# A fused linear-attention and mixer kernel on one core: the first batch's value tiles from GpSimd's DMA queue

## The chip, the cores and the metric

The kernel runs on one core of a Trainium2 chip. A core has TensorE (PE in the profile; PEld are its weight loads), VectorE (DVE), ScalarE (ACT), GpSimd (POOL) and SyncE (SP), which run side by side and wait for each other by semaphores. Transfers between the chip's memory (HBM) and the core's on-chip memory are issued by one of these engines and carried out by 16 DMA engines. The metric is device microseconds (us) of one execution; times are medians of several runs.

## The reference

Two blocks follow each other. The first is a gated linear attention over 4 batches, 8 heads, 768 steps and 48 channels:

```python
f = 1.0 / (1.0 + np.exp(-f_logit))
for t in range(S):
    state = f[:, :, t, :, None] * state + np.einsum('bhd,bhe->bhde', k[:, :, t], v[:, :, t])
    y[:, :, t] = np.einsum('bhd,bhde->bhe', q[:, :, t], state)
```

The second takes its output, as 4 x 768 x 384, through a low-rank mixing of the steps and two dense layers:

```python
u  = x + (x.transpose(0, 2, 1) @ U @ V).transpose(0, 2, 1)      # U 768x32, V 32x768
ch = np.maximum(u @ w_ch1, 0.0) @ w_ch2                         # 384x1536, 1536x384
out = u + ch
```

The inputs q, k, v and f_logit are float32. The weights arrive in a 64-bit form and are converted on the core.

## The kernel before

A unit is one pair of heads of one batch; there are 16, and units 0 to 3 (HP is 4) are the first batch. For each unit the kernel loads the gate logits f, the keys k, the queries q and the values v. The values go into tiles of their own, of which three exist; f, k and q go into two slots that alternate, so unit n+2 reuses what unit n has read:

```python
v_tiles[n] = three.tile([P, NBL, 2, D], F32, name="v_nat")
nat[n % 2][nm]                     # slots "late" (even units) and "other" (odd units)

def load(n, *names):
    b, hp = divmod(n, HP)
    for nm in names:
        if nm == "v":
            v_tiles[n] = three.tile([P, NBL, 2, D], F32, name="v_nat")
        for par in range(2):                       # the two heads of the pair
            head = src[nm][b, 2 * hp + par]
            if nm == "v" and par:
                for s in range(2):                 # the second head's halves are swapped: two transfers
                    nc.sync.dma_start(
                        out=v_tiles[n][(1 - s) * C : (2 - s) * C, :, par, :],
                        in_=head.rearrange("(c s p) d -> s p c d", s=2, p=C)[s],
                    )
                continue
            if nm == "v" or n < TURNED:
                dst = v_tiles[n] if nm == "v" else nat[n % 2][nm]
                nc.sync.dma_start(out=dst[:, :, par, 0:D], in_=head.rearrange("(c p) d -> p c d", p=P))
                continue
            # ... later units: finer transfers in another layout

load(0, "f", "k", "q")
load(1, "f")
load(0, "v")
load(1, "k", "q", "v")
```

A transfer of one head is 128 partitions by 6 rows of 48 float32, so it is made of pieces of 192 bytes. After these loads GpSimd fills constants and clears buffers, ending with a few small ones:

```python
nc.gpsimd.memset(added[:, 0:1], 0.0)
for i in range(2):
    nc.gpsimd.memset(wholes[i][:, 0:1], 0.0)
```

The work on a unit has these parts:

```python
# front of a unit
pt = on_tensor("f")                                  # TensorE transposes f into a PSUM tile
nc.scalar.activation(halves(f)[:, :, :, 1:C], pt[:, :, :, 1:C], AF.Sigmoid)
nc.vector.tensor_tensor_scan(...)                    # suffix products of the gates (keep)
nc.vector.tensor_tensor(halves(t), on_tensor("k"), halves(T["X"]), ALU.mult)
nc.vector.tensor_tensor_scan(Y, f[:, 0:S], starts, 0.0, ALU.mult, ALU.add)
nc.vector.tensor_tensor(halves(t), on_tensor("q"), halves(T["Y"]), ALU.mult)
# rear of a unit
nc.tensor.transpose(...)                             # kept: the keys back, by chunks
nc.tensor.matmul(ds[...], lhsT=T["kb"][...], rhs=vt[...])      # states: keys by VALUES
nc.vector.tensor_tensor_scan(states, added, whole, 0.0, ALU.add, ALU.mult)
nc.tensor.matmul(sc[...], lhsT=T["k"][...], rhs=T["q"][...])   # scores
nc.vector.tensor_tensor(T["A"], sc, causal, ALU.mult)
nc.tensor.matmul(y[...], lhsT=T["q"][...], rhs=T["st"][...])   # read
nc.tensor.matmul(y[...], lhsT=T["A"][...], rhs=vt[...])        # inner: scores by VALUES
```

The first batch's units follow each other in this loop, which also issues the later loads; the order of TensorE, VectorE and ScalarE is kept as written, and a scheduler places SyncE's and GpSimd's instructions:

```python
for n in range(HP):
    pieces = front(n, "keep", "keys") + rear(n - 1, "scan", "scores")
    pieces += [lambda: busy(3)] + rear(n, "kept") + front(n, "read_back", "queries")
    if n + 1 < HP:
        pieces += front(n + 1, "gates") + rear(n - 1, "read", "inner") + rear(n, "states")
    for piece in pieces:
        piece()
    if n < 2:
        load(n + 2, "v")
    if n == 1:
        for start, _ in weights[: early + 2]:        # U, V and two blocks of w_ch1
            start()
    elif n > 1:
        load(n + 2, "f", "k", "q", "v")
```

f, k and q of unit n+2 are loaded as soon as unit n has read its own. busy(3) are three matmuls without use, to keep TensorE occupied. Each weight is loaded, then converted by two ScalarE, three VectorE and one GpSimd operation (lines 90 to 95). Each load on a queue has one of eight semaphores, and waits for the load that had the semaphore before.

## Time and profile before

| What | Value |
|---|---|
| Time, median of 3 runs | 488.54 us (488.51 to 489.53) |
| Span of the profiled execution | 486.9 us |
| TensorE granted clock | 0.998 of full |
| DMA moved | 34.34 MB, mean 71 GB/s |
| DMA pieces under 512 B | 149206 of 158679 |
| Value loads v_nat | 16 of 144 KB, 32 of 72 KB, all from SyncE |
| Small clearings on GpSimd end | 5.4 us |
| GpSimd idle after them | 36.87 us, until the first weight is converted at 42.29 us |

The page has busy times by engine, the span in 40 slices with a digit for the busy tenths of each, the DMA queues, the chain of work that ended last, and groups of instructions. In the table of stretches DMA's share can pass 1, since pieces of a transfer overlap in an engine. In the timeline a line gives start, length, engine, source line, operation, output and inputs, and in brackets the idle time before it and what ended it. "issue" stands for idle time in which the engine waited for nothing that the profile shows. SPq is SyncE's queue of transfers; its times are those of the issue, and the data land later.

### The profile page before, as it was taken

The numbers are of one execution on the slowest core, as the hardware profiler recorded it, in microseconds if no ns is written. First come the engines' busy times: TensorE is split into PE (matmuls) and PEld (weight loads), VectorE is DVE, ScalarE is ACT, GpSimd is POOL, SyncE is SP. The second block draws the span as 40 slices with busy tenths as digits, with TensorE's granted clock in tenths as the row PEclk, the third lists the DMA queues.
The fourth block names the chain that finished last, engine by engine and source line by source line (L and its number), as shares of the span: only waits on it lengthen the run. The fifth ranks groups of instructions, "written<-read, shape, count | busy, mean of one in ns | idle before, by whom it ended". The sixth has DMA issues, their size and how long they took to land.

```text
span 486.9 us, 12734 instructions
## 1 busy us (share of the span) xinstructions
PE 469.2 (96%) x5541; PEld 400.0 (82%) x5541; DVE 355.4 (73%) x563; ACT 163.2 (34%) x309; POOL 37.6 (8%) x49
## 2 busy tenths in 40 slices
PE   7996899999999999999999999999999999999995
PEld 4775688886566568899898888899979999999995
DVE  5887689777999857656857548797896886958642
ACT  2444666664334313423231403433231312112200
POOL 3002245453000000000000000000000000000000
PEclk9999999999999999999999999999999999999999
DMA  9979975756778512333535100100000000000001
GB/s 146 158 153 178 254 194 135 162 143 79 110 116 121 96 41 36 52 48 67 76 55 94 25 18 18 27 3 20 19 1 1 33 2 18 16 1 34 1 33 38
DMA packets 158679, 34.34 MB, mean 71 GB/s; under 512 B 149206, under 2 KB 157078, under 8 KB 158614
## 3 DMA queue, kind: packets, MB, share of 16 engines
q1 hardware_dynamic: 158614, 33.44, 37.0%
q8 instruction: 45, 0.74, 0.6%
q14 instruction: 20, 0.16, 0.1%
HBM read 28.70 MB, written 4.72 MB: 69 GB/s over the span
## 4 chain that ended last, share of the span: by engine, by line
PE 79%; DVE 10%; DMA 3%; issue 3%; ACT 2%; SPq 2%; DVEq 0%; ACTq 0%
PE pw L312 26%; PE pz L258 23%; PE pp L410 11%; PE y L863 2%; PE pt L660 2%; PE sc L788 2%; PE ds L825 2%; PE y L881 2%; PE po L283 2%; PE idle L962 2%; PE put L246 1%; DMA late<-in_f_logit_dram 1%; DVE late L694 1%; DVE late L712 1%; PE pt L809 1%
## 5 line engine op out<-in xcount | busy, mean ns | idle before, releaser
L258 PE MATMUL pz<-uT,w 128*128 128x256 f32 x504 | 115.7, 383 | 0.3 <-ACT uT L247 0.3
L258 PEld LDWEIGHTS pz<-uT,w 128*128 128x128 f32 x504 | 93.4, 190 | 13.3 <-issue 0.5
L312 PE MATMUL pw<-w,z_all 128*128 128x192 f32 x216 | 37.7, 329 | 0.0
L312 PE MATMUL pw<-zw,w_raw 128*128 128x192 f32 x216 | 37.4, 327 | 0.0
L312 PEld LDWEIGHTS pw<-zw,w_raw 128*128 128x128 f32 x216 | 35.2, 190 | 0.8 <-issue 0.6
L312 PEld LDWEIGHTS pw<-w,z_all 128*128 128x128 f32 x216 | 35.0, 190 | 0.7
L95 POOL TENSOR_TENSOR w<-w_y,w_r 128x384 int32<-128x384 int32 x24 | 31.5, 1311 | 41.5 <-DVE w_y L94 36.5
L694 DVE TENSOR_TENSOR_SCAN late<-fz,late 128x768 f32<-128x768 f32 x16 | 28.1, 1755 | 8.9 <-ACT fz L689 4.2
L268 ACT ACTIVATE z_all<-pz 128x512 f32<-128x512 f32 x33 | 19.7, 596 | 41.4 <-PE pz L258 41.3
L410 PE MATMUL pp<-v_nat,late 128*128 128x128 f32 x224 | 28.8, 275 | 0.0
L712 DVE TENSOR_TENSOR_SCAN late<-fz,other 128x768 f32<-128x768 f32 x16 | 27.9, 1745 | 0.1
L410 PEld LDWEIGHTS pp<-v_nat,late 128*128 128x128 f32 x224 | 27.0, 192 | 0.0
L283 PE MATMUL po<-w,zw 128*128 128x384 f32 x72 | 25.6, 499 | 0.0
L283 PE MATMUL po<-w,z_all 128*128 128x384 f32 x72 | 25.3, 496 | 0.3 <-DVE o L187 0.3
L403 ACT ACTIVATE other<-other 128x512 f32<-128x512 f32 x18 | 11.3, 631 | 39.9 <-DVE other L187 39.9
L851 ACT COPY st<-added 128x576 f32<-128x576 f32 x12 | 14.7, 1224 | 27.5 <-DVE added L846 27.5
L92 DVE TENSOR_SCALAR w_y<-w_y 128x384 f32<-128x384 f32 (+3 forms) x27 | 13.1, 485 | 14.0 <-ACT w_y L90 13.8
L795 DVE TENSOR_TENSOR A<-sc,causal 128x768 f32<-128x768 f32 x16 | 15.2, 947 | 10.7 <-PE sc L788 10.7
L283 PEld LDWEIGHTS po<-w,z_all 128*128 128x128 f32 x72 | 13.1, 190 | 8.7 <-DVE o L187 0.9
L283 PEld LDWEIGHTS po<-w,zw 128*128 128x128 f32 x72 | 12.9, 189 | 8.7 <-issue 1.2
L187 DVE TENSOR_TENSOR w_raw<-z_all 128x768 f32<-128x768 f32 x12 | 11.4, 954 | 10.6 <-ACT z_all L268 9.2
L312 PE MATMUL pw<-w,other 128*128 128x192 f32 x108 | 18.6, 327 | 0.0
(193 smaller groups left out, 825.6 us busy)
## 6 DMA issues: line engine op xcount, KB each, us to landing
w_raw<-in_moe_w_ch_dram SPq DMA_DIRECT2D x18, 384.0 KB, 3.9
out_dram<-o SPq DMA_DIRECT2D x24, 192.0 KB, 1.9
v_nat<-in_v_dram SPq DMA_DIRECT2D x16, 144.0 KB, 3.6
v_nat<-in_v_dram SPq DMA_DIRECT2D x32, 72.0 KB, 3.3
zw<-in_moe_w_ch_dram SPq DMA_DIRECT2D x6, 384.0 KB, 5.7
late<-in_f_logit_dram SPq DMA_DIRECT2D x10, 96.0 KB, 3.1
late<-in_k_dram SPq DMA_DIRECT2D x10, 96.0 KB, 3.0
late<-in_q_dram SPq DMA_DIRECT2D x10, 96.0 KB, 2.6
```

Source lines behind the costliest of these rows:

```text
L92: nc.vector.tensor_scalar(f, f, SMALLEST, LARGEST, ALU.max, ALU.min)
L95: nc.gpsimd.tensor_tensor(dst.bitcast(I32), shaped(y.bitcast(I32)), shaped(r), ALU.add)
L187: nc.vector.tensor_tensor(*args)
L258: nc.tensor.matmul(pm[:, i * 2 * P : (i + 1) * 2 * P], lhsT=w1[:, m, o : o + P], rhs=uT[a][:, m, :], start=(m == 0), stop=(m == NDC - 1))
L268: nc.scalar.activation(z[a, c][:, k : k + 2, :].rearrange("p i t -> p (i t)"), pm, AF.Relu)
L283: nc.tensor.matmul(pm, lhsT=z[a, i // NI][:, i % NI, s * P : (s + 1) * P], rhs=w2[:, i, :], start=(i == 0), stop=(i == NFC - 1))
L312: nc.tensor.matmul(pm[:, n * HM : (n + 1) * HM], lhsT=lhs[:, i, :], rhs=rhs[:, i, :], start=(i == 0), stop=(i == NI - 1))
L410: nc.tensor.matmul(pm[:, i, r * P : (r + 1) * P], lhsT=room["w"](wn)[:, r * P : (r + 1) * P], rhs=x_node(a, xn), start=((xn, wn) == of[0]) ...
L694: nc.vector.tensor_tensor_scan(backwards(X, S - 1, S), backwards(f, S, S), backwards(ends, S - 1, S), 0.0, ALU.mult, ALU.add,)
L712: nc.vector.tensor_tensor_scan(Y, f[:, 0:S], starts, 0.0, ALU.mult, ALU.add)
L795: nc.vector.tensor_tensor(T["A"], sc[:, :, 0 : NBL * C].rearrange("p h (c i) -> p h c i", i=C), causal.unsqueeze(1).unsqueeze(1).broadcast ...
L851: nc.scalar.copy(st, states.rearrange(by_e, c=NCH))
```

## The change

The value tiles of units 0 to 3 are issued from GpSimd instead of SyncE, twelve transfers in all. Those of units 0 and 1 are moved behind GpSimd's clearings in the program, so that they don't hold these up; those of units 2 and 3 are called where they were. All else stays with SyncE, whose queue now has fewer loads in front of the f, k and q that follow. The sizes and the layout of the transfers are the same.

```diff
+            queue = nc.gpsimd if nm == "v" and n < HP else nc.sync
             for par in range(2):
                 head = src[nm][b, 2 * hp + par]
                 if nm == "v" and par:
                     for s in range(2):
-                        nc.sync.dma_start(
+                        queue.dma_start(
                             out=v_tiles[n][(1 - s) * C : (2 - s) * C, :, par, :],
                             in_=head.rearrange("(c s p) d -> s p c d", s=2, p=C)[s],
                         )
                     continue
                 if nm == "v" or n < TURNED:
                     dst = v_tiles[n] if nm == "v" else nat[n % 2][nm]
-                    nc.sync.dma_start(out=dst[:, :, par, 0:D], in_=...)
+                    queue.dma_start(out=dst[:, :, par, 0:D], in_=...)
                     continue
...
     load(0, "f", "k", "q")
     load(1, "f")
-    load(0, "v")
-    load(1, "k", "q", "v")
+    load(1, "k", "q")
...
     for i in range(2):
         nc.gpsimd.memset(wholes[i][:, 0:1], 0.0)
+    load(0, "v")
+    load(1, "v")
```

The lines of the kernel below the change move down by two or three.

## The prediction

> **What bounds the kernel now.** I read the page first, then the table of stretches, then the chain of work that ended last in order of time up to 60 us, then the timeline of the same stretch. From the page:

> ```profile
> PE 469.2 (96%) x5541; PEld 400.0 (82%) x5541; DVE 355.4 (73%) x563; ACT 163.2 (34%) x309; POOL 37.6 (8%) x49
> ...
> DMA  9979975756778512333535100100000000000001
> ...
> q8 instruction: 45, 0.74, 0.6%
> ```

> TensorE is busy nearly throughout; DMA is full only in the first slices (12.2 us each). The twelve value transfers that change queue all lie there. In the table of stretches TensorE is busy for 61.67 of the 62 us from 55 to 117, and after 117 us the DMA share is 0.23. So only the first 55 us matter, and what is won or lost in them should move the end by as much. The same table for the start (stretch, length, busy us and counts of PE, PEld, DVE, ACT and POOL, clock, DMA share, GB/s):

> ```profile
> 5.00:10.00 5.00, 4.61 (x16) 3.33 (x15) 2.78 (x5) 1.59 (x4) 0.42 (x6) 1.00 1.49 170
> 10.00:15.00 5.00, 5.00 (x82) 3.68 (x80) 3.43 (x4) 2.40 (x5) 0.00 (x0) 1.00 1.46 165
> 15.00:20.00 5.00, 4.49 (x74) 2.94 (x73) 4.93 (x8) 1.36 (x4) 0.00 (x0) 1.00 1.23 160
> 20.00:25.00 5.00, 4.72 (x174) 4.16 (x175) 4.65 (x7) 2.73 (x7) 0.00 (x0) 1.00 0.78 133
> 25.00:30.00 5.00, 5.00 (x82) 3.59 (x78) 4.90 (x5) 1.60 (x3) 0.00 (x0) 1.00 0.88 149
> ```

> Two things are to be seen. DMA moves 165 to 170 GB/s until about 15 us with a share above 1, so it is full: a second queue cannot make it faster, only reorder it. And from 15 us VectorE is busy for 4.65 to 4.93 of each 5 us, so the units of batch 0 go at VectorE's pace (its suffix scans start at 14.47, 22.34 and 30.71 us: some 8 us a unit), as long as no load comes late. One load is at that edge, in the chain:

> ```profile
> 14.68 5.21 DMA late<-in_f_logit_dram
> 19.89 0.14 issue
> 20.02 0.85 PE pt L660 x6
> ```

> Unit 2's gate logits are issued from SyncE at 14.09 and 14.68 us, land at 19.89, and TensorE transposes them 0.13 us later. The timeline shows how near the other conditions are:

> ```profile
> 19.99 0.64 PEld L660 LDWEIGHTS pt<-ident,late 128*128 128x128 f32 x6 [0.74 <-DVE A L795]
> 20.02 0.85 PE L660 MATMUL pt<-ident,late 128*128 128x128 f32 x6 [0.53 <-DMA late<-in_f_logit_dram]
> ...
> 20.90 0.80 ACT L681 ACTIVATE fz<-pt 128x756 f32<-128x756 f32 x1 [0.59 <-PE pt L660]
> ...
> 22.34 1.75 DVE L694 TENSOR_TENSOR_SCAN late<-fz,late 128x768 f32<-128x768 f32 x1
> ```

> The sigmoid ends at 21.70 us and VectorE takes the scan at 22.34, when it has finished its product of the queries (21.46 plus 0.96 us). So unit 2's gates have 0.64 us of slack and no more. The value tiles have little either: unit 0's are first read at 13.46 us (state matmuls, L825), and their transfers are issued at 6.25 to 8.80 us and take 3.8 to 4.7 us to land.

> Later there are two holes on TensorE with no cause that the profile names:

> ```profile
> 42.13 0.74 PE L788 MATMUL sc<-qT,kz 48*64 48x64 f32 x34 [1.72 <-issue]
> ...
> 46.86 1.16 PE L208 MATMUL ph<-x,U 128*32 128x288 f32 x11 [1.94 <-issue]
> ```

> I take them for waits for TensorE's instructions. The page's q8 carries 45 pieces and 0.74 MB, about 16 KB each; 2 x 5541 matrix instructions over 45 are some 246 to a piece; and by the table of stretches TensorE starts 127 matmuls and 127 weight loads from the end of the first hole to that of the second. The matmuls here are small, so a piece is used up in a few us.

> [...]

> **The change part by part.** Removed from SyncE: 12 issues; those of units 0 and 1 take 0.81, 1.69, 0.84 and 1.49 us in SyncE's timeline, 4.8 together, so some 9.7 us for four units. That is no time on the path by itself, since SyncE's issues were slow because DMA was full.

> Added on GpSimd: 12 issues, starting after its last small memset at about 5.4 us. It is idle from there to 42.29 us (its first weight addition waited 36.87 us), so the issuing itself costs nothing there. I have no duration for it; I assume 0.7 to 1.5 us each. Units 0, 1 and 2 follow without a wait; unit 3 waits for unit 0's tile, which is free at about 23.2 us.

> Moved: the built order of SyncE's instructions. Before, it is (f0 is f of unit 0) f0 k0 q0 f1 v0 k1 q1 v1 f2 k2 q2 f3 v2 k3 q3 v3, then U, V and the first layer's weights. After, it is f0 k0 q0 f1 k1 q1 U f2 k2 V q2 f3 k3, three blocks of weights, q3, then f4. The scheduler has filled the gaps with weights. So two kinds of bytes come ahead of f2 that were behind it: U, and unit 2's values, which GpSimd hands out early.

> The sum for f2: one tensor of one unit is 2 x 144 KB, 0.295 MB. Before, nine of them end with f2: 2.65 MB. At 165 GB/s that is 16.1 us; DMA starts at about 1.8 us, so 17.9, and f2 landed at 19.89, so 2.0 us are latency. After, if the two queues share evenly from about 7 us, 1.38 MB of SyncE's (f1 k1 q1 U f2) stand beside 0.885 MB of GpSimd's (v0 v1 v2), which is the smaller, so all of it is done first. Thus 0.197 MB (U) and 0.295 MB (v2) are added: 0.49 MB / 165 GB/s = 3.0 us. f2 lands at 22.9, the slack of 0.64 is used up, and unit 2's scan is 2.3 us late. VectorE has no room to win that back before 40 us.

> Other loads by the same count: k1 at about 15.2 instead of 13.5 us; its product on VectorE runs at 16.63, the transposes need 0.9, so it just fits. q2, f3, k3 and q3 come to 27.7, 30, 33 and 38 us against needs (2.3 us later than before) of 30.6, 31.2, 35.1 and 39.5. They fit. v0, handed out from 5.4 to 9 us and sharing, lands at 13 to 14.5 against 13.46; a lag of about 1.4 us is swallowed, since the next VectorE work that depends on what follows is at 16.63.

> At 36 to 47 us the loads differ from before: more weights are in by then, with larger pieces, so the instruction fetches may have to wait less. Of the 3.7 us of holes I count 0.5 to 1 us won, but with little confidence, as the same bytes still have to come before about 55 us. Weights themselves gain nothing: ScalarE's first conversion at 40.30 us stands behind unit 2 and 3 work in its own order.

> Sum: +2.3 for f2, -0.7 for the holes, -0.3 because GpSimd may hand out more slowly than an even share: +1.3 us. 488.5 + 1.3 = 489.8 us.

> **The rivals.** First, the loads of f, k, q do come earlier, as the change means, because GpSimd gets a smaller share or two queues move more in all. For it: in the first 4 us the slices of DMA show about 200 GB/s, above the later 165. Against it: U goes ahead in any case, 1.2 us. The most to be had at f2 is 0.3 us (20.02 against 19.69, when VectorE had left the buffer, 18.76 plus 0.93 us); the rest would have to come from the holes, up to 3.4 us: 485.5 to 488 us. Second, GpSimd is slow at issuing[...]: v0 lands at 16 to 20 us, the state matmuls stop TensorE, and its in-order queue delays everything behind by 1 to 5 us: 490 to 494 us. [...] Third, all is hidden: 488.5 us. This needs v2 to stay behind f2; then only U's 1.2 us come ahead, of which 0.64 is slack, and the holes give back the rest.

> **Range and chances.** 2% is 9.8 us. To reach it either way would take more than all holes together (3.7 us) or a v0 that lands 11 us late. I take 486.8 to 492.4 us for 8 in 10: below it the first rival at its best, above it the second. Faster by over 2%: 0.015, slower: 0.025, within: 0.96.

> **What would show it.** Right: f2's transposes at 22 to 23.5 us with a wait for its DMA of some 2 us, unit 2's scan near 24.5, DMA still full at 20 us, w1 blocks landing before 40. Wrong: f2 landing before 20 us, or v0's matmuls well after 13.5 us with TensorE waiting for the value tile; holes at 40 to 47 us gone or doubled; or a changed length after 55 us.

## The result, and the profile after

| | before | after |
|---|---|---|
| Time, median of 4 runs | 488.52 us (487.26 to 489.53) | 496.44 us (495.45 to 496.90) |
| Ratio, 95% interval | | 1.0161 (1.0132 to 1.0189) |
| Span of the profile | 486.9 us | 494.6 us |
| Mean granted TensorE clock in it | 0.998 | 0.984 |

The change costs 7.9 us, nearly all of it early. The first matmul of the dense layers (pz) starts at 62.88 us instead of 55.84. From there to the start of the last matmul it takes 425.35 us (425.32 before), and what follows that matmul is 0.5 us longer.

The page of the kernel after, for the lines that were shown of before; in the DMA queues q0 is GpSimd's:

```profile
PE 473.4 (96%) x5541; PEld 403.3 (82%) x5541; DVE 355.9 (72%) x563; ACT 163.3 (33%) x309; POOL 46.1 (9%) x61
...
PEclk9859999999999999999999999999999999999999
DMA  9999826757577714251625300100000000000001
...
q1 hardware_dynamic: 152278, 32.26, 35.1%
q0 software_dynamic: 640, 1.18, 1.3%
q8 instruction: 45, 0.74, 0.6%
```

The instructions are the same (GpSimd's twelve more are the issues), and TensorE is busy 4.2 us longer. The line PEclk has an 8 and a 5 in the second and third slice (12.4 to 37.1 us). In the page of the kernel before it was full:

```profile
PEclk9999999999999999999999999999999999999999
```

The table of stretches of the kernel after (stretch, length, busy us and counts of PE, PEld, DVE, ACT and POOL, clock, DMA share, GB/s) shows it closer:

```profile
10.00:15.00 5.00, 4.34 (x99) 3.65 (x101) 4.58 (x4) 2.58 (x5) 1.97 (x3) 1.00 1.36 166
15.00:20.00 5.00, 4.12 (x68) 2.63 (x59) 4.93 (x8) 1.58 (x3) 0.00 (x0) 1.00 1.28 167
20.00:25.00 5.00, 2.19 (x34) 1.89 (x38) 1.27 (x2) 0.63 (x1) 0.00 (x0) 0.67 0.95 150
25.00:30.00 5.00, 4.74 (x130) 4.41 (x122) 2.18 (x4) 1.79 (x6) 2.10 (x3) 0.50 0.79 153
30.00:35.00 5.00, 5.00 (x55) 3.22 (x54) 4.64 (x4) 0.67 (x1) 0.05 (x1) 0.50 1.06 270
35.00:40.00 5.00, 4.74 (x128) 3.65 (x128) 2.47 (x3) 1.84 (x4) 0.00 (x0) 0.96 1.08 179
```

Until 20 us all is nearly as before: DMA still moves 166 GB/s, VectorE is busy for 4.93 us. Then VectorE falls to 1.27 us where it had 4.65, and TensorE, once it has work again, does it at a clock of 0.50: 130 matmuls fill 4.74 us. The clock's records give one spell, from 21.7 us on, 13.65 us long. The chain that ended last, in order of time, in the kernel after:

```profile
14.80 7.87 DMA late<-in_f_logit_dram
22.81 1.52 PE pt L663 x6
24.33 1.48 PE y L866 x44
...
31.81 3.93 PE idle L965 x6
```

The chain goes through the same load as before, unit 2's gate logits, which lands at 22.67 us. Then it stays on TensorE, through every small group of matmuls and even the useless ones (L965). It did so in the kernel before too, where the same pieces were shorter:

```profile
20.87 1.19 PE y L863 x43
...
25.72 2.13 PE idle L962 x6
```

So VectorE alone had not set the pace, although it was busy for 4.65 and 4.90 us of the two stretches from 20 us: TensorE was busy for 4.72 and 5.00. In the timeline of the kernel before VectorE twice waits a little for what TensorE's transposes feed, once directly and once through the sigmoid:

```profile
24.75 0.96 DVE L672 TENSOR_TENSOR kz<-pt,late 128x768 f32<-128x768 f32 x1 [0.17 <-PE pt L660]
...
30.71 1.76 DVE L694 TENSOR_TENSOR_SCAN late<-fz,late 128x768 f32<-128x768 f32 x1 [0.16 <-ACT fz L681]
```

Both engines were nearly full, and a slower TensorE had no room. The timeline of the kernel after:

```profile
5.39 0.98 POOL L550 DMA_DIRECT2D v_nat<-in_v_dram  x1
...
13.07 0.89 PE L828 MATMUL ds<-v_nat,kb 64*64 64x48 f32 x42 [0.34 <-DMA v_nat<-in_v_dram]
...
15.56 2.20 PE L965 MATMUL idle<-late,ident 128*128 128x384 f32 x6
...
22.81 1.52 PE L663 MATMUL pt<-ident,late 128*128 128x128 f32 x6 [2.85 <-DMA late<-in_f_logit_dram]
...
25.20 1.76 DVE L697 TENSOR_TENSOR_SCAN late<-fz,late 128x768 f32<-128x768 f32 x1 [3.83 <-ACT fz L684]
...
27.90 0.84 POOL L550 DMA_DIRECT2D v_nat<-in_v_dram  x1 [15.93 <-PE y L884]
...
31.74 4.00 PE L965 MATMUL idle<-late,ident 128*128 128x384 f32 x6
...
38.59 1.76 DVE L697 TENSOR_TENSOR_SCAN late<-fz,late 128x768 f32<-128x768 f32 x1 [0.53 <-ACT fz L684]
```

TensorE waits 2.85 us for the logits. The useless matmuls of one busy(3), six records in the profile, take 2.20 us at 15.56 and 4.00 us at 31.74: that is the half clock, read from one instruction. Unit 2's scan comes at 25.20 (22.34 before) and unit 3's at 38.59 (30.71 before): 2.9 us late have become 7.9 within one unit.

The records of the clock show 1.00 or 0.50, and in all the profiles below the low spells before 70 us last 3.41 us or a multiple of it. How long TensorE was busy just before a fall differs. In one experiment (sync_late) it did nothing in the 3.4 us before the fall. But here it was busy for 0.85 us of them before the fall at 21.7 us, and in another (v01_order) for 2.16. The executions of one kernel scatter: over 38 executions of the kernel before, of 486.7 to 492.9 us, the time goes with the mean granted clock by 3.04 us for each 0.01 (r = -0.82). A hundredth of a mean over 487 us is 9.7 us at half clock, so each us at half clock goes with about 0.31 us of time. This is a correlation: a stall can lengthen an execution and lower its clock at once, as the wait of 2.70 us does in fill4 below.

### The profile page after: what moved, and what is told of

The parts are those of the page before. It is cut to its first block, busy times and chain, and to the rows that moved or that the text cites. A ratio compares the mean times of both kernels' runs of the same rounds, so it can differ in the third digit from the quotient of the medians.

```text
span 494.6 us, 12747 instructions
## 1 busy us (share of the span) xinstructions
PE 473.4 (96%) x5541; PEld 403.3 (82%) x5541; DVE 355.9 (72%) x563; ACT 163.3 (33%) x309; POOL 46.1 (9%) x61
## 3 DMA queue, kind: packets, MB, share of 16 engines
q1 hardware_dynamic: 152278, 32.26, 35.1%
HBM read 28.70 MB, written 4.72 MB: 68 GB/s over the span
## 4 chain that ended last, share of the span: by engine, by line
PE 78%; DVE 9%; DMA 4%; issue 3%; SPq 2%; ACT 2%; POOL 1%; DVEq 0%; POOLq 0%; ACTq 0%
PE pw L312 25%; PE pz L258 23%; PE pp L410 11%; PE y L866 2%; DMA late<-in_f_logit_dram 2%; PE sc L791 2%; PE ds L828 2%; PE y L884 2%; PE pt L663 2%; PE po L283 2%; PE put L246 1%; DVE late L715 1%; PE idle L965 1%; DMA v_nat<-in_v_dram 1%; PE pt L812 1%
## 5 line engine op out<-in xcount | busy, mean ns | idle before, releaser
L95 POOL TENSOR_TENSOR w<-w_y,w_r 128x384 int32<-128x384 int32 x24 | 31.2, 1299 | 41.0 <-DVE w_y L94 33.0
L798 DVE TENSOR_TENSOR A<-sc,causal 128x768 f32<-128x768 f32 x16 | 15.2, 948 | 10.0 <-PE sc L791 10.0
L884 PEld LDWEIGHTS y<-v_nat,A 64*64 64x64 f32 x768 | 13.4, 140 | 6.6 <-ACT seen L873 3.4
```

The lines of the kernel that those rows point to most:

```text
L95: nc.gpsimd.tensor_tensor(dst.bitcast(I32), shaped(y.bitcast(I32)), shaped(r), ALU.add)
L798: nc.vector.tensor_tensor(T["A"], sc[:, :, 0 : NBL * C].rearrange("p h (c i) -> p h c i", i=C), causal.unsqueeze(1).unsqueeze(1).broadcast ...
L884: nc.tensor.matmul(o(s, par, c), lhsT=T["A"][part[s ^ par], par, c, :], rhs=vt[part[s ^ par], c, par, :], start=False, stop=True, skip_gro ...
```

## The experiments

The theory: unit 2's late logits leave TensorE idle for 2 to 3 us, which halves its clock, and that multiplies a lateness of 2.5 us. The rivals: GpSimd's queue costs something itself; the scheduler's new order of SyncE (weights between the units' loads) does; the holes in TensorE's instructions do. Intervals are at 95%; ratios are to the kernel before, run beside each. A profile shows one execution, which is often not the median one.

**sync_late: the lateness, without GpSimd.** The kernel before, all loads from SyncE in a fixed order, with unit 2's values and U moved ahead of its gate logits.

```diff
+load(2, "v")
+weights[0][0]()
 busy(1)
 ...
-    if n < 2:
+    if n == 1:
         load(n + 2, "v")
     if n == 1:
-        for start, _ in weights[: early + 2]:
+        for start, _ in weights[1 : early + 2]:
```

> The kernel before, all loads on SyncE, but unit 2's values and U are put ahead of unit 2's gate logits, as many bytes as the change put there; the order of SyncE's loads is fixed until the first batch's loop ends. Theory (a late f2, and then a halved TensorE clock): f2 lands at 22 to 23.5 us, TensorE is idle for 2.5 to 3 us, the granted clock falls to 0.5 until about 36 us, and the time is 495 to 498 us. Rival (GpSimd's queue itself slows loads[...]): nothing of this, 488 to 490.5 us.

Measured: 493.39 us, ratio 1.0081 (1.0060 to 1.0103). Its timeline:

```profile
22.48 1.51 PE L660 MATMUL pt<-ident,late 128*128 128x128 f32 x6 [3.62 <-DMA late<-in_f_logit_dram]
...
24.86 1.76 DVE L694 TENSOR_TENSOR_SCAN late<-fz,late 128x768 f32<-128x768 f32 x1 [3.60 <-ACT fz L681]
...
35.51 1.76 DVE L694 TENSOR_TENSOR_SCAN late<-fz,late 128x768 f32<-128x768 f32 x1
```

Transposes at 1.51 us again, a spell of half clock from 22.4 us for 6.83, unit 3's scan 4.8 us late. A second spell of 6.83 us starts at 56.51. So the lateness and the fall of the clock need no GpSimd. Together they make 4.8 us of the 7.9, less than the 495 to 498 us that were expected.

**fill4: no idle time ahead of the late logits.** The kernel after, with four useless matmuls more in the place of the wait.

```diff
 pieces += [lambda: busy(3)] + rear(n, "kept") + ...
+if n + 1 == 2:
+    pieces += [lambda: busy(4)]
 if n + 1 < HP:
     pieces += front(n + 1, "gates") + ...
```

> The changed kernel with four more useless matmuls (some 2.9 us) ahead of unit 2's gate transposes, so that TensorE isn't idle while f2 is on its way. Theory: f2 still lands at 22 to 23.5 us, but the clock stays at 1.0, unit 3's suffix scan starts near 33.5 instead of 38.6 us, and the time is 490 to 492 us. Rival (the loads after f2, k2 to q3, come late and set the pace, not the clock): unit 3's scan stays at 37 to 39 us, 495 to 497 us.

Measured: 497.38 us, ratio 1.0148 (1.0058 to 1.0237). The table of stretches of fill4:

```profile
25.00:30.00 5.00, 5.00 (x156) 3.90 (x156) 4.17 (x7) 1.75 (x4) 2.14 (x3) 1.00 0.90 169
30.00:35.00 5.00, 4.74 (x156) 4.05 (x156) 4.86 (x5) 2.43 (x6) 0.00 (x0) 1.00 1.11 241
35.00:40.00 5.00, 2.30 (x78) 1.92 (x70) 2.62 (x5) 1.76 (x4) 0.00 (x0) 0.94 1.01 214
40.00:45.00 5.00, 5.00 (x22) 2.56 (x18) 2.62 (x2) 0.00 (x0) 0.00 (x0) 0.50 1.06 249
```

And its timeline:

```profile
24.36 1.76 DVE L697 TENSOR_TENSOR_SCAN late<-fz,late 128x768 f32<-128x768 f32 x1 [3.07 <-ACT fz L684]
...
33.17 1.76 DVE L697 TENSOR_TENSOR_SCAN late<-fz,late 128x768 f32<-128x768 f32 x1
...
39.69 0.48 PE L791 MATMUL sc<-qT,kz 48*64 48x64 f32 x4 [2.70 <-issue]
```

The first half came as the theory has it: the clock is 1.00 in unit 2, and from unit 2's scan to unit 3's are 8.8 us (13.4 in the kernel after, 8.4 before). The time did not: at 37 us TensorE waits 2.7 us for its own instructions, and the clock falls in that wait, at 39.4 us, for 6.83 us. The expected 490 to 492 us were missed. The profile is one of two executions at some 499 us; the two others took 495.8 at a mean clock of 0.992. So even with less time at half clock (0.984 in the kernel after) the time was much that of the kernel after: the expected gain went into other waits, this one among them.

**order: SyncE's order as before.** The kernel after with SyncE's instructions in the order of the program text; the values of all four units still come from GpSimd.

```diff
+with tc.manual_schedule(engines={nc.sync.engine}):
     busy(1)
     ...                                  # the loop over the four units, unchanged
```

> The changed kernel with SyncE's order fixed as written during the first batch's loop, so U and all weights come behind q3; GpSimd still loads the values of units 0 to 3. Theory: U's 0.197 MB are gone from ahead of f2, which lands at 21 to 22 us; TensorE is idle for about 1.6 us; if that is too short for the clock to fall, 488.5 to 490.5 us, if it isn't, 493 to 495. Rival (GpSimd's queue itself): 493 to 496 us with the clock at 1.0.

Measured: 496.37 us, ratio 1.0112 (1.0017 to 1.0207). The logits' transposes start at 21.98 us with a wait of 2.22, and a spell of half clock of 10.24 us follows. The median is above what either reading had expected (488.5 to 496 us). It is not the weights, then, that make most of the lateness, but the values that GpSimd hands out early. The interval is wide; order_again below repeats the run.

**v01_order: GpSimd for units 0 and 1 alone.** As order, with the values of units 2 and 3 back on SyncE.

```diff
-queue = nc.gpsimd if nm == "v" and n < HP else nc.sync
+queue = nc.gpsimd if nm == "v" and n < 2 else nc.sync
```

> As the last, but only the values of units 0 and 1 are loaded from GpSimd, those of units 2 and 3 from SyncE behind f3 and q3. The same bytes stand ahead of f2 as in the kernel before. Theory: f2 lands at 19.5 to 20.5 us, the clock stays at 1.0, 487.5 to 489.5 us. Rival (GpSimd's queue itself): f2 lands later than 20.5 us or VectorE's work is longer, 490 us or more.

Measured: 488.68 us, ratio 1.0003 (0.9985 to 1.0021). Its timeline:

```profile
20.18 0.85 PE L663 MATMUL pt<-ident,late 128*128 128x128 f32 x6 [1.38 <-DMA late<-in_f_logit_dram]
...
21.90 1.76 DVE L697 TENSOR_TENSOR_SCAN late<-fz,late 128x768 f32<-128x768 f32 x1 [0.52 <-ACT fz L684]
```

Six of the twelve transfers come from GpSimd and the logits are on time: no cost, within 0.2%. GpSimd's queue by itself is free here. The execution of this profile, 491.98 us, is the second longest of twenty. It had a short fall all the same, 3.41 us from 22.6 on, with a wait of only 1.38 us ahead of it.

**after_again: the kernel after, unedited.**

> The changed kernel once more, without an edit, to see how its time goes with the granted clock from execution to execution. Theory (the late f2 costs some 2 to 3 us, the halved clock the rest): executions with a mean clock of 0.99 or more are at 490 to 494 us, those at 0.984 at 495 to 497, so that a line through them meets 1.0 near 489 to 491. Rival (a loss that has nothing to do with the clock): time and clock aren't tied, and all executions are at 495 to 497 us.

Measured: 496.51 us, ratio 1.0153 (1.0121 to 1.0186). The profile has half clock from 23.1 us for 6.83 and from 50.4 for 6.83, where the first had 13.65 in one piece; unit 3's scan is at 35.76 instead of 38.59, but the dense layers start at 63.83. So the place of the spells changes from one execution to the next, while both profiles have 13.65 us of them before 70 us; by the mean clocks of the ten executions (0.979 to 0.991) it is an estimated 9 to 21 us. The expectation that a line through the executions meets the full clock at 489 to 491 us failed: it meets it at 493.2, on six points. By that more than half of the loss would be there without the half clock.

**nofill2: without the useless matmuls of units 2 and 3.**

```diff
-pieces += [lambda: busy(3)] + rear(n, "kept") + ...
+pieces += [lambda: busy(3 if n < 2 else 0)] + rear(n, "kept") + ...
```

> The changed kernel without the three useless matmuls in units 2 and 3. In the changed kernel's profile those of unit 2 took 4.0 us of TensorE at the halved clock, where VectorE waited for TensorE. Theory (the halved clock makes TensorE the limit of unit 2): unit 3's suffix scan starts 2 to 3.5 us earlier than in the changed kernel (at 35 to 36.5 us) if the clock falls as there, and the time is 492.5 to 495.5 us. Rival (loads set the pace): the scan stays at 38 to 39 us, time 495 to 497.

Measured: 494.92 us, ratio 1.0130 (1.0094 to 1.0167), against 1.0153 for after_again beside it: not told apart by the intervals. The 4.00 us of useless work are gone, and the profile has 20.5 us at half clock, in four spells. Unit 3's scan comes at 35.95 us, as expected; but in after_again, without the edit, it came at 35.76, so the earlier scan can't be put down to the edit.

**v1_behind: unit 2's logits earlier than before.** The kernel before with unit 1's values loaded after unit 0's gates are issued, all from SyncE in fixed order.

```diff
-load(1, "k", "q", "v")
+load(1, "k", "q")
 ...
 for piece in front(0, "gates"):
     piece()
+load(1, "v")
```

> The kernel before, all loads on SyncE, but unit 1's values come behind unit 2's gate logits: 0.295 MB less ahead of f2. Theory: f2 lands near 18 us, TensorE no longer waits for it, unit 2's scan is VectorE's alone to set (22.0 to 22.4 us), the clock falls in fewer executions, and the time is 486.5 to 488.5 us. Rival (f2 isn't what matters at this place): same as before, 488 to 490 us, with the same spread.

Measured: 488.17 us, ratio 0.9993 (0.9969 to 1.0017). Its timeline:

```profile
18.78 0.88 PE L660 MATMUL pt<-ident,late 128*128 128x128 f32 x6
...
21.37 1.75 DVE L694 TENSOR_TENSOR_SCAN late<-fz,late 128x768 f32<-128x768 f32 x1
```

The transposes no longer wait, 1.24 us earlier than before. The profiled execution is 1.7 us shorter and the shortest of its kernel, but over 12 executions nothing is left of it. Earlier logits are worth little; late ones cost much.

**v01_fill2: v01_order with two useless matmuls ahead of unit 2's gates**, against its 1.38 us of waiting.

```diff
+    if n + 1 == 2:
+        pieces += [lambda: busy(2)]
```

> Values of units 0 and 1 from GpSimd, those of 2 and 3 from SyncE behind f3 and q3, SyncE's order fixed, and two more useless matmuls (1.5 us) ahead of unit 2's gate transposes. Theory: f2 lands at 19.5 to 20.5 us, the wait of 1.4 us is filled, the clock doesn't fall at 22 us, and the time is 487 to 488.5 us with fewer slow executions. Rival (instruction holes at 36 to 47 us lower the clock anyway): 489 to 492 us, with the fall at 40 us or later.

Measured: 489.84 us, ratio 1.0029 (1.0014 to 1.0044). The profile has no fall before 46.05 us, and one there, as the rival had it. The time is 0.3% above the kernel before and not better than v01_order's: the filling does not pay.

Open after these were two things: why sync_late cost 4.8 us and the change 7.9, and why filling the gap won nothing. Four more runs followed.

**sync_late_fill4: sync_late with the four matmuls of fill4**, the same edit.

> sync_late (all loads from SyncE, unit 2's values and U ahead of its gate logits) with four useless matmuls more on TensorE just ahead of unit 2's gate transposes. If the late logits cost mainly through the granted clock: no spell of half clock from 20 to 36 us, unit 3's suffix scan at 33 to 33.5 us instead of 35.51, median about 490 (the full-clock end of sync_late's line was 490.04). If the clock is only a by-product: the extra matmuls win nothing, median 493 to 494 as in sync_late.

Measured: 497.11 us, ratio 1.0161 (1.0121 to 1.0200). Full clock from 20 to 38.8 us and unit 3's scan at 33.26 us, as the theory had it; the 490 us were missed by 7. The four matmuls did not only win nothing, they cost: sync_late's ratio was 1.0081 (1.0060 to 1.0103). Its timeline shows where part of it went:

```profile
39.26 0.48 PE L788 MATMUL sc<-qT,kz 48*64 48x64 f32 x3 [2.18 <-issue]
39.66 4.21 PE L962 MATMUL idle<-late,ident 128*128 128x384 f32 x6
```

The wait for instructions is at the same matmuls as in fill4 (the scores), and the clock falls in it, at 38.8 us, so that the useless ones take 4.21 us.

**order_fill4: order with the four matmuls.**

> order (values from GpSimd, SyncE's order as before) with the same four useless matmuls. Theory, late logits and clock: no spell of half clock before 36 us, unit 3's scan at 32.5 to 33.5 us instead of 36.91, median 489 to 492. Rival, values from GpSimd cost something that neither the clock nor the lateness holds: median 493 or more, clearly above sync_late_fill4 in this call.

Measured: 496.45 us, ratio 1.0162 (1.0135 to 1.0189). Unit 3's scan at 33.47 us and no fall before 52.5, as expected; the time again is not. It is above 493, as the rival had it, but not above sync_late_fill4, so the rival's reason (GpSimd) falls too. It is 0.5 us above order_again, which had 17.07 us at half clock in its profile where order_fill4 had 3.41.

**v012_order: unit 3's values back on SyncE**, that is order with `n < 3`.

> order with unit 3's values back on SyncE; units 0, 1 and 2 stay on GpSimd. Theory: unit 2's values, handed out early, are the cause; logits of unit 2 land near 22 us, half clock follows, median 493 to 497. Rival, the wait of GpSimd for unit 0's tile and the late values of unit 3 cost the rest: median near sync_late's 493.4 or below, order above it by 2 us or more.

Measured: 494.09 us, ratio 1.0100 (1.0070 to 1.0131). The transposes start at 21.71 us after a wait of 1.99. Unit 2's values without U make most of the lateness.

**order_again: order, unedited.**

> order, unedited, for a narrower interval (it was 496.37 from 4 executions, 492.48 to 497.82) beside the three others. Theory: 493.5 to 497, the spread along the line of 3 us for each 0.01 of mean granted clock. Rival, the scheduler's order of SyncE is half of the change's cost: 491 to 493.

Measured: 495.94 us, ratio 1.0128 (1.0084 to 1.0171). With the first run order's ratio is 1.011 and 1.013, near the change itself; its interval overlaps with v012_order's, so a share of unit 3's values is neither shown nor excluded.

## Where the time is, over all profiles

Three things can be read from each profile: how much later than before unit 2's transposes start; the sum of four holes in TensorE's instructions; and the time at half clock before 70 us. A hole is the time from the start of one record to that of the next behind the 961st, 1217th, 1473rd and 1729th record of TensorE: its matmuls, weight loads and semaphore instructions counted together (256 apart; by matmuls and weight loads alone, 253 or 254). The count is the same in every kernel: when fill4 put matmuls in, the holes came at other matmuls and at the same count. Half clock counts at 0.31 us each. The last column is the start of the last matmul, against before's 481.16 us.

| kernel | transposes later | holes (before: 4.58) | half clock | sum | last matmul |
|---|---|---|---|---|---|
| after | +2.79 | 3.72 | 13.65 | +6.2 | +7.1 |
| after_again | +2.70 | 5.44 | 13.66 | +7.8 | +8.0 |
| order | +1.96 | 4.71 | 17.07 | +7.4 | +8.2 |
| order_again | +2.00 | 4.27 | 17.07 | +7.0 | +8.0 |
| v012_order | +1.69 | 4.83 | 6.82 | +4.1 | +4.3 |
| sync_late | +2.46 | 3.15 | 13.66 | +5.3 | +6.0 |
| fill4 | +2.63 | 6.05 | 13.66 | +8.3 | +9.6 |
| sync_late_fill4 | +2.54 | 5.87 | 13.66 | +8.1 | +8.9 |
| order_fill4 | +2.43 | 6.22 | 3.41 | +5.1 | +5.8 |
| nofill2 | +2.67 | 3.76 | 20.47 | +8.2 | +6.6 |
| v01_order | +0.16 | 5.00 | 6.82 | +2.7 | +3.1 |
| v01_fill2 | +0.25 | 3.57 | 3.41 | +0.3 | +0.5 |
| v1_behind | -1.24 | 3.33 | 0.00 | -2.5 | -1.8 |

An example, after: 2.79 + (3.72 - 4.58) + 0.31 x 13.65 = 6.2. The sum comes within 1.3 us of the last matmul in all but nofill2, which has less work to do. In all the others it is too short, by 0.2 to 1.3 us. It is a reckoning made after the fact, and late transposes and half clock mostly come together in it, so it can't tell their shares apart; but no kernel needs a fourth term for GpSimd. Why the change cost 7.9 us and sync_late 4.8, with nearly the same lateness and the same 13.66 us at half clock in the profiles, stays open.

The holes are waits for instruction fetches, as far as the traces show it. The page's q8, of the kind "instruction", has 45 pieces, each of 16384 bytes in the trace, and in the kernels before and after one of them lands 1.35 to 1.63 us before TensorE goes on behind the 1217th, the 1473rd and the 1729th record. I call the 256 records from one such count to the next a block, by the number of its first. In fill4 block 961 starts at 34.01 us and needs 2.8 us of execution; the fetch for block 1217 runs from 37.00 to 38.32, and the block starts at 39.69. In the kernel before the block starts at 31.66, the fetch runs from 33.32 to 34.24, and the next block starts at 35.84, 0.30 us after the matmuls ran out. From the start of a block to the start of the next, by way of the fetch, this takes 5.7 us in fill4 and, with the 1.3 to 1.6 us that pass between landing and start where TensorE waits, an estimated 4 us in the kernel before. So the block that was executed in 2.8 us was followed by a wait of 2.70, and the one whose execution took 3.9 by one of 0.30. What varies is when the fetch begins: 1.7 us after the block's start in the kernel before, 3.0 in fill4, 3.3 in v01_order (from 33.21 to 36.53 us). From 32 to 34 us DMA moved 132 GB/s in the kernel before, and from 34 to 36 us 299 in fill4 and 300 in v01_order, when weights were on the way. That this traffic is what delays the fetch is argued from these numbers; no run moved the weights alone, and sync_late's fetch began 1.1 us after its block's start at 36.46 us, while DMA moved 192 GB/s from 36 to 38 (fill4 had 199).

## The prediction, step by step

**f2's landing: right.** 22.9 us predicted, 22.67 measured, with a wait of 2.85 us on TensorE and DMA full up to 20 us (a share of 1.28 from 15 us on). That the two queues share evenly was an assumption of the sum; in the trace GpSimd's moved 0.55 MB from 9 to 15 us and SyncE's 0.46. The two added kinds of bytes were right. Their shares were counted as 1.8 us for unit 2's values and 1.2 for U; without U ahead the lateness is still 1.69 us (v012_order) to 2.00 (order_again) of 2.79.

**Unit 2's scan: nearly.** Predicted was "2.3 us late"; it was 2.86 late, because the six transposes ran 1.52 us instead of 0.85, at half clock.

**The pace after it: wrong, and this is the step that failed.** The sum took "+2.3 for f2" to the end of the kernel as it stood, on the ground that "the units of batch 0 go at VectorE's pace". TensorE was as full, and the chain of before ran on it with the useless matmuls: the slack of 0.64 us was VectorE's and spared TensorE nothing, and a slower TensorE made the unit longer at once (13.4 us from scan to scan, 8.4 before). In the trace of after VectorE is busy for only 1.27 and 2.18 us of the two stretches from 20 us. TensorE at half clock sets the pace, and the 2.86 us are 7.88 at unit 3's scan. The three runs with the four matmuls confirm this much: with full clock in unit 2, unit 3's scan is 2.5 to 2.8 us late. The wait was sized as time lost, and not as idle time with a slower TensorE after it (transposes of 1.52 us instead of 0.85).

How much of the whole loss is the clock's is argued, not shown, since the same three runs were no faster. For after_again against the kernel before beside it, 8.4 us apart: 2.7 us of lateness in the profile; the clock, a median of 0.985 instead of 0.997, at 3.04 us for each 0.01 another 3.6; the end of the program after the last matmul 0.6 longer in the profiles; together 6.9. Some 1.5 us stay without a name.

**GpSimd: right.** Its issues took 0.98 and 0.84 us for 144 KB and 0.66 for 72 KB (0.7 to 1.5 assumed); v0 landed at 13.02 us (13 to 14.5), and TensorE waited 0.34 us for it. The second rival had the size (490 to 494, nearer than my 489.8) for a reason that these numbers and v01_order disprove. The other loads fitted, save that TensorE waited 0.84 us for unit 1's queries at 19.12, while VectorE was still busy.

**The holes, -0.7: no step to rely on.** In the profile after they are 0.86 us shorter, in after_again 0.86 longer. The reason given, that larger pieces of weights let fetches through sooner, has fill4's numbers against it.

**The range: wrong for the same reason.** It listed waits only: "more than all holes together (3.7 us) or a v0 that lands 11 us late". 492.4 us as the upper end left no room for a clock that falls, though the page of before has the line for it. The length after 55 us did not change, as said.

## What to carry to other kernels

Where a load's slack is under a microsecond and TensorE has little work around it, count a late landing not as its own length alone: add up how long TensorE then idles in a stretch of 3.4 us, the shortest spell of half clock here. In these profiles 1.0 us of it could bring a spell of 3.4 to 14 us at half clock for the small matmuls behind it, and from 1.8 us on one always came. Look also whether TensorE is on the chain there, as it was here. A second queue here did not only add an issuer, it let bytes that nobody needed yet (0.295 MB of unit 2's values) overtake those on the path, unit 2's gate logits, which TensorE then took up 1.69 to 2.00 us later even without U ahead; leave on it what is needed first (v01_order costs nothing) and keep later tiles behind. And useless matmuls in the gap held the clock at 1.00 in unit 2, but the three kernels with four of them were no faster (ratios of 1.0148 to 1.0162): the time went into later stalls, the instruction fetch among them.
